# Spreading one row over 128 partitions: from a selector matmul to two DMAs by way of DRAM

## The chip, the cores and the metric

The kernel runs on one core of one Trainium2 chip. The metric is device time in microseconds (us) of one execution. The kernel before was timed three times: 608.44, 608.82 and 608.91 us, median 608.82. A separate profiled execution of the same kernel took 607.33 us.

The five engines of the core have the short names of the profile: PE (TensorE, with its weight loads as PEld), DVE (VectorE), ACT (ScalarE), POOL (GpSimd) and SP (SyncE, which here only issues stores). DMAs are issued by POOL, SP and ACT, each from its own queue.

## What is computed

```python
X = np.fft.fft(x, axis=1)          # x: 8 x 3008 x 256, float32
X = np.fft.fft(X, axis=2)
t = X.real.reshape(8 * 3008, 256)
h = np.maximum(t @ w_in, 0.0)      # w_in: 256 x 2048
return (h * h) @ w_out             # w_out: 2048 x 256
```

A real two-dimensional Fourier mixing, then a feed-forward layer with a squared ReLU.

## The kernel before

**Folding the transforms.** Both transforms are sums of cosines and sines of real data, so the kernel computes row k and row S-k of the output together: the cosine part is common, the sine part changes its sign. `zc` holds the cosine part of such a pair and `zs` the sine part, both 128 partitions (index d of the model dimension) by columns (the pairs k). The transform over d is multiplied into `w_in` once, which gives the weights `gh[:, 0]` (for `zc`), `gh[:, 1]` (for `zs`) and `gh[:, 2]` (minus two times `gh[:, 1]`). There are 129 cosine indices d and 128 partitions; the sine of d = 0 is zero, so partition 0 of `zs` carries the cosine row d = 128 instead. That row must not change its sign with the rest, and this is what the change is about.

**Windows and steps.** The 12,040 pair columns are cut into 25 windows, most of 512 columns. A window w is worked off in eight steps s = 0 to 7 (`NST`), each of which makes two of the sixteen 128-row chunks of h for both rows of every pair. In every step PE also runs 16 matmuls of line 687 (`ffn2_steps`), the second product of the window before; its results are copied by ACT (L702) and stored by SP (L667). Some jobs of the next windows are spread over the steps by hand: the matmuls of line 572 that make `zc` and `zs` of the next window (`z_steps`, run in steps `lo` to `hi - 1`), their evacuation by ACT (L577, L583) and DVE (L601), and the folds of x on DVE. The program is written out in the order in which each engine executes it; nothing reorders it.

**Two kinds of step.** In an ordinary step PE makes cosine plus sine part (L829, L830), ACT applies the ReLU (L861) for row k, PE adds `gh[:, 2]` times `zs` (L852), and ACT applies the ReLU for row S-k. In a step that is listed in `diff[w]` (steps 4 and 6 at first, then mostly 0, 2, 4, 6; the windows of the folds have fewer) the second row comes without the extra matmuls:

1. PE makes the cosine part alone (L838, `cosines`).
2. DVE computes t2 = n2 - 2 times the cosine part (L842, `twice`).
3. PE adds the sine part in place (L847, `sines`), which must wait for `twice`, as both use the same PSUM tile.
4. ACT takes the ReLU for row k (L861), and DVE adds t2 for row S-k (L859).

Here `n2` is the correction for d = 128: the row in partition 0 of `zs`, spread over all 128 partitions as tile `zn`, times one number per row of h (`g2n`). POOL makes it (L790, `nyq_rows`, two instructions for a step).

**The spread.** `spread_nyq(wt)` makes `zn` for window wt. It multiplies `zs` by the 128 x 128 matrix `sel`, which is 1 in row 0 and 0 elsewhere (L781, one matmul of up to 512 columns into a `ps_z` tile), and ACT copies the result to SBUF (L782). It is called 21 times, once for each of windows 4 to 24, from `nyq` (L892) near the end of the window before, at step `hi`; `hi` is 5 when window w+1 has 0 in its list, else 6. Window 4 makes its own in step 0. `nyq_rows` for the first listed step follows in the same step, those for the others in the steps after. The `n2` tiles share three buffers. POOL's queue also holds the write of the folded rows to DRAM (L456), their read-back (L464, L466) and the loads of x (L127, L132), in the program's order.

Of the kernel before, what the change touches and what calls it, by code (L numbers as in the profile page):

```python
# [9 lines left out]
F32 = mybir.dt.float32  # L10
F16 = mybir.dt.float16
I32 = mybir.dt.int32
AF = mybir.ActivationFunctionType
# [3 lines left out]
P = 128  # L17
# [12 lines left out]
def kernel(  # L30
# [14 lines left out]
    nc = tc.nc  # L45
    B, S, D = x.shape
# [9 lines left out]
    WN = 512  # L56
# [25 lines left out]
    def win_of(col):  # L82
        return max(w for w in range(NW) if wins[w][0] <= col) if col < TOT else NW
# [5 lines left out]
    col_of = {}  # L89
# [11 lines left out]
    const = ctx.enter_context(tc.tile_pool(name="const", bufs=1))  # L101
# [9 lines left out]
    drp = ctx.enter_context(tc.tile_pool(name="drp", bufs=2, space=bass.MemoryType.DRAM))  # L111
    ps_h = ctx.enter_context(tc.tile_pool(name="ps_h", bufs=2, space=bass.MemoryType.PSUM))
    ps_o = ctx.enter_context(tc.tile_pool(name="ps_o", bufs=2, space=bass.MemoryType.PSUM))
    ps_z = ctx.enter_context(tc.tile_pool(name="ps_z", bufs=2, space=bass.MemoryType.PSUM))
# [201 lines left out]
    for i in (1, 0):  # L316
        nc.gpsimd.tensor_scalar(out=perm[i], in0=prow_i, scalar1=float(P - 1 - i), scalar2=None, op0=ALU.is_equal)
    nc.gpsimd.dma_start(out=wout16, in_=moe_w_out.rearrange("(c p) o -> p c o", p=P))
    sel = const.tile([P, P], F16, name="sel")
    nc.gpsimd.memset(sel, 0.0)  # L320
    nc.gpsimd.memset(sel[0:1, :], 1.0)
    pick = const.tile([P, 1], F16, name="pick")
    nc.gpsimd.memset(pick, 0.0)
    nc.gpsimd.memset(pick[0:1, :], -2.0)
# [42 lines left out]
    def fold_steps(i):  # L367
# [130 lines left out]

        late = [lambda: fold8(0), lambda: fold8(1), lambda: fold16(0), lambda: fold16(1), nyq8]
        return {"u_odd": u_odd, "u_part": u_part, "v_even": v_even, "v_part": v_part, "d_even": d_even, "n_cos": n_cos, "odds": odds, "d_odd": d_odd, "load": load, "n_sin": n_sin, "nyq": nyq, "even": even, "away": away, "back": back, "late": late}  # L500

    gh = const.tile([P, 3, F], F16, name="gh")
# [35 lines left out]
    def zwin(w):  # L538
        if w not in zc:
            zc[w] = zp.tile([P, WN], F16, name="zc", tag="zc")  # L540
            zs[w] = zp.tile([P, WN], F16, name="zs", tag="zs")
        return zc[w], zs[w]
# [182 lines left out]
    NST = NFC // 2  # L725
    at_of = {w: [[] for _ in range(NST)] for w in range(NW)}
    post_of = {w: [[] for _ in range(NST)] for w in range(NW)}
    diff = {w: (0, 2, 4, 6) if w > 5 else (4, 6) for w in range(4, NW)}
# [35 lines left out]
    n2s = {}  # L764
# [12 lines left out]
    def spread_nyq(wt):  # L777
        wn1 = wins[wt][1]
        zn = zns[wt] = znp.tile([P, WN], F16, name="zn", tag="zn")
        pn = ps_z.tile([P, 512], F32, name="pn", tag="pz")  # L780
        nc.tensor.matmul(pn[:, 0:wn1], sel, zwin(wt)[1][:, 0:wn1], start=True, stop=True)  # L781
        nc.scalar.activation(zn[:, 0:wn1], pn[:, 0:wn1], AF.Copy, bias=0.0, scale=1.0)  # L782

    def nyq_rows(wt, steps):
        wn1 = wins[wt][1]
        for s in steps:
            n2 = n2s[wt, s] = wp.tile([P, 2, WN], F32, name="n2", tag="w16")
            for a in range(2):
                fc = 2 * s + a
                nc.gpsimd.tensor_scalar(out=n2[:, a, 0:wn1], in0=zns[wt][:, 0:wn1], scalar1=g2n[:, fc : fc + 1], scalar2=1.0, op0=ALU.mult, op1=ALU.mult)  # L790

    old = None
    for w in range(NW):
# [1 line left out]
        h2 = h2p.tile([P, NFC, 2 * WN], F16, name="h2", tag="h2")  # L795
        zcw, zsw = zwin(w)

        lo, hi = int(any(win_of(col_of[i, 1]) == w + 1 for i in range(2, B))), NST - 3 if 0 in diff.get(w + 1, ()) else NST - 2
        at, post = at_of[w], post_of[w]
        if w == 1:  # L800
            fj = fold_jobs(1)
# [6 lines left out]
        elif w == 3:  # L808
# [4 lines left out]
            lo, hi = 3, NST - 1  # L813
        elif w == win_of(col_of[1, 1]) - 1:
            for st in range(5):
                at[min(st, 3)] += folds[1]["late"][st : st + 1]
            lo, hi = 4, NST - 1
# [74 lines left out]
        def nyq(s):  # L892
            if w + 1 in diff and hi < NST - 1:
                if s == hi:
                    spread_nyq(w + 1)
                    nyq_rows(w + 1, diff[w + 1][0:1])
                elif s == hi + 1:
                    nyq_rows(w + 1, diff[w + 1][1 : 2 if s < NST - 1 else None])
                elif s == hi + 2:
                    nyq_rows(w + 1, diff[w + 1][2:])  # L900
            if s == 0 and w in diff and w not in zns:
                spread_nyq(w)
                nyq_rows(w, diff[w])

        def quad(p):
            ph = phs[p] = ps_h.tile([P, 2, 512], F32, name="ph", tag="psh")
            for c in range(4):
                f0 = (4 * p + c) * P
                o = ph[:, c // 2, (c % 2) * wn : (c % 2 + 1) * wn]
                nc.tensor.matmul(o, gh[:, 0, f0 : f0 + P], zcw[:, 0:wn], start=(c % 2 == 0), stop=False, skip_group_check=True)  # L910
                nc.tensor.matmul(o, gh[:, 1, f0 : f0 + P], zsw[:, 0:wn], start=False, stop=True, skip_group_check=True)
# [54 lines left out]
        for s in range(NST) if w > 1 else ():  # L966
            held["on"] = s + 1 in diff.get(w, ()) or (s + 1 == NST and 0 in diff.get(w + 1, ()))
            if s in diff.get(w, ()):
                cosines(s)
                twice(s)  # L970
                settle()
                others(s)
                sines(s)
                first(s)
                relu(s, 1)
                keep(s, 1, 2)
                plus.append(lambda s=s, p=power_act: p(s))
                nyq(s)
                continue
            pq(s)  # L980
            settle()
            first(s)
            if s == NST - 1:
                power(s, 0, 1)
            others(s)
            nyq(s)
            turn(s)
            relu(s, 1)
            keep(s, int(s == NST - 1), 2)
# [36 lines left out]
```

## Time and profile before

| | |
|---|---|
| timed, median of three | 608.82 us |
| profiled execution, its own time | 607.33 us |
| its span | 605.5 us |
| PE busy | 591.2 us, 98% of the span |
| DVE, ACT, POOL busy | 490.1, 462.8, 213.6 us |
| mean granted TensorE clock | 0.999 |
| spread matmuls (L781) | 21, median 379 ns each |
| their copies (L782, ACT) | 21, median 608 ns each |
| rows of n2 (L790, POOL) | 146, median 692 ns, longest 2444 ns |

The duration of a matmul in the profile is that of one instruction from its start to its modelled end. Matmuls are pipelined, so the rate is read from the distance between the starts of two that follow each other: 0.21 us for 512 columns.

### The profile page before, as it was taken

How to read it: one execution, taken by the hardware profiler on the slowest of the kernel's cores; microseconds unless marked ns; L12 is line 12 of the kernel's file. 1: busy time of each engine (PE TensorE's matmuls, PEld its weight loads, DVE VectorE, ACT ScalarE, POOL GpSimd, SP SyncE). 2: the span in 40 equal slices, each digit the busy share in tenths (PEclk: the TensorE clock that was granted, in tenths of full speed). 3: DMA queues.
4: the chain of work that ended last, by engine and by line, in shares of the span. 5: the costliest groups of instructions: out<-in, count | busy, mean ns of one | idle time of the engine just before them, and what ended most of it. 6: DMA issues, size and time to landing. Idle time of an engine off the chain costs nothing.

```text
span 605.5 us, 11294 instructions
## 1 busy us (share of the span) xinstructions
PE 591.2 (98%) x4449; PEld 427.9 (71%) x4449; DVE 490.1 (81%) x593; ACT 462.8 (76%) x634; POOL 213.6 (35%) x249
## 2 busy tenths in 40 slices
PE   7899999999999999999999999999999999999997
PEld 3457786776777777777777767777677777777786
DVE  8787656987998878979889799888988988777760
ACT  6697777968888787877787878787777787878762
POOL 8320223245504506365045451363431522513300
PEclk9999999999999999999999999999999999999999
DMA  8945321127111361271113711146112311111112
GB/s 150 155 90 136 115 71 34 39 94 150 52 49 40 114 140 52 77 166 48 52 37 109 146 53 36 40 125 134 44 30 86 88 35 39 51 46 38 54 57 69
DMA packets 36524, 47.52 MB, mean 78 GB/s; under 512 B 4215, under 2 KB 30327, under 8 KB 36471
## 3 DMA queue, kind: packets, MB, share of 16 engines
q0 software_dynamic: 9344, 22.14, 17.9%
q1 hardware_dynamic: 26899, 24.44, 13.5%
q8 instruction: 35, 0.57, 0.4%
q10 hardware_dynamic: 228, 0.21, 0.1%
q14 instruction: 18, 0.15, 0.1%
HBM read 33.63 MB, written 27.84 MB: 102 GB/s over the span
## 4 chain that ended last, share of the span: by engine, by line
PE 87%; DVE 9%; ACT 2%; issue 1%; POOL 0%; DVEq 0%; POOLq 0%; ACTq 0%
PE po L687 49%; PE ph L852 8%; PE ph L829 7%; PE ph L830 7%; PE ph L847 5%; PE ph L838 5%; PE pz L572 4%; DVE h L868 3%; DVE t L842 2%; DVE h L859 2%; DVE xy L491 1%; PE pn L781 1%; ACT h L923 1%; ACT h L861 0%; DVE m L243 0%
## 5 line engine op out<-in xcount | busy, mean ns | idle before, releaser
L687 PE MATMUL po<-wout,h 128*128 128x256 f16 (+1 forms) x3024 | 362.3, 273 | 0.0
L861 ACT ACTIVATE h<-ph 128x1024 f16<-128x1024 f32 (+3 forms) x311 | 295.5, 993 | 79.0 <-PE ph L847 59.1
L687 PEld LDWEIGHTS <-h 128*128 128x128 f16 (+1 forms) x3024 | 296.8, 98 | 72.0
L790 POOL TENSOR_SCALAR n<-zn,g2n 128x512 f32<-128x512 f16 (+2 forms) x146 | 144.2, 1002 | 256.3 <-ACT zn L782 248.4
L868 DVE TENSOR_TENSOR h<-h 128x1024 f16<-128x1024 f16 (+6 forms) x216 | 203.2, 951 | 30.0 <-ACT h L861 27.5
L859 DVE CUSTOM_DVE_ANT_0 h<-t,ph 128x1024 f16<-128x1024 f32 x67 | 81.7, 1220 | 31.6 <-ACT h L861 31.5
L842 DVE SCALAR_TENSOR_TENSOR t<-ph,n 128x1024 f32<-128x1024 f32 (+2 forms) x73 | 87.7, 1202 | 23.4 <-PE ph L838 22.1
L829 PE MATMUL ph<-zc,gh 128*128 128x512 f16 (+3 forms) x238 | 87.4, 368 | 0.4 <-ACT h L923 0.3
L830 PE MATMUL ph<-zs,gh 128*128 128x512 f16 (+3 forms) x238 | 87.4, 368 | 0.0
L872 ACT ACTIVATE h<-h 128x1024 f16<-128x1024 f16 (+2 forms) x73 | 76.5, 1048 | 0.0
L852 PE MATMUL ph<-zs,gh 128*128 128x512 f16 (+3 forms) x238 | 68.1, 368 | 0.2 <-ACT h L861 0.2
L702 ACT ACTIVATE osb<-po 128x512 f32<-128x512 f32 (+3 forms) x95 | 55.5, 589 | 10.6 <-PE po L687 9.7
L847 PE MATMUL ph<-zs,gh 128*128 128x512 f16 (+2 forms) x146 | 42.7, 374 | 1.4 <-DVE t L842 1.2
L838 PE MATMUL ph<-zc,gh 128*128 128x512 f16 (+2 forms) x146 | 42.8, 375 | 0.4 <-DVE h L859 0.4
L830 PEld LDWEIGHTS <-gh 128*128 128x128 f16 x238 | 23.2, 98 | 25.7 <-issue 0.9
L829 PEld LDWEIGHTS <-gh 128*128 128x128 f16 x238 | 23.2, 97 | 25.0
L577 ACT ACTIVATE es<-pz 128x376 f32<-128x376 f32 (+1 forms) x32 | 14.9, 486 | 16.4 <-PE pz L572 16.3
L852 PEld LDWEIGHTS <-gh 128*128 128x128 f16 x238 | 22.3, 98 | 6.2 <-issue 0.3
L838 PEld LDWEIGHTS <-gh 128*128 128x128 f16 x146 | 14.3, 98 | 17.2 <-issue 0.6
L456 POOL DMA_DIRECT2D scr<-ev x8 | 4.9, 616 | 58.3 <-DVE ev L452 52.5
L466 POOL DMA_INDIRECT rb<-scr,idx_r x16 | 18.2, 1140 | 4.9 <-issue 4.9
L132 POOL DMA_INDIRECT xo<-in_x_dram,idx_r x15 | 16.3, 1090 | 4.5 <-issue 4.3
(145 smaller groups left out, 368.5 us busy)
## 6 DMA issues: line engine op xcount, KB each, us to landing
out_dram<-osb SPq DMA_DIRECT2D x77, 128.0 KB
xo<-in_x_dram POOLq DMA_DIRECT2D x7, 768.0 KB
scr<-ev POOLq DMA_DIRECT2D x8, 390.0 KB, 2.9
rb<-scr POOLq DMA_DIRECT2D x16, 130.0 KB
out_dram<-osb SPq DMA_DIRECT2D x12, 94.0 KB
w<-in_moe_w_in_dram POOLq DMA_DIRECT2D x2, 512.0 KB
wout<-in_moe_w_out_dram POOLq DMA_DIRECT2D x1, 1024.0 KB, 11.9
out_dram<-osb SPq DMA_DIRECT2D x8, 75.0 KB
```

The source lines that it names most:

```text
L687: nc.tensor.matmul(po[0:m, j * D : (j + 1) * D], h2[:, fc, q : q + m], wout16[:, fc, :], start=(fc == 0), stop=(fc == NFC - 1))
L790: nc.gpsimd.tensor_scalar(out=n2[:, a, 0:wn1], in0=zns[wt][:, 0:wn1], scalar1=g2n[:, fc : fc + 1], scalar2=1.0, op0=ALU.mult, op1=ALU.mult)
L829: nc.tensor.matmul(ph[:, a, 0:wn], gh[:, 0, f0 : f0 + P], zcw[:, 0:wn], start=True, stop=False)
L830: nc.tensor.matmul(ph[:, a, 0:wn], gh[:, 1, f0 : f0 + P], zsw[:, 0:wn], start=False, stop=True)
L838: nc.tensor.matmul(ph[:, a, 0:wn], gh[:, 0, f0 : f0 + P], zcw[:, 0:wn], start=True, stop=True)
L842: nc.vector.scalar_tensor_tensor(out=t2[:, :, 0:wn], in0=phs[s][:, :, 0:wn], scalar=-2.0, in1=n2s[w, s][:, :, 0:wn], op0=ALU.mult, op1=ALU ...
L847: nc.tensor.matmul(phs[s][:, a, 0:wn], gh[:, 1, f0 : f0 + P], zsw[:, 0:wn], start=False, stop=True, skip_group_check=True)
L852: nc.tensor.matmul(phs[s][:, a, 0:wn], gh[:, 2, f0 : f0 + P], zsw[:, 0:wn], start=False, stop=True, skip_group_check=True)
L859: nc.vector._custom_dve(TENSOR_ADD_SAT, out=h, in0=t2s[s][:, :, 0:wn], in1=phs[s][:, :, 0:wn], s0=BIG, s1=0.0)
L861: nc.scalar.activation(h, phs[s][:, :, 0:wn], AF.Relu, bias=0.0, scale=-1.0)
L868: nc.vector.tensor_tensor(h, h, h, op=ALU.mult)
L872: nc.scalar.activation(h, h, AF.Square, bias=0.0, scale=1.0)
```

## The change

`sel` goes. `spread_nyq` writes the row (1 x 512 f16, 1 KB) from partition 0 of `zs` to a DRAM tile `rd` with a DMA on ACT's queue, and a DMA on POOL's queue reads that row back into all 128 partitions of `zn`, with a stride of 0 over the partitions. POOL's DMA waits for the landing of ACT's, and `nyq_rows` for the landing of POOL's.

The calls move as well. `hi` becomes one smaller wherever window w+1 has `diff` steps: 4 (0 in its list) or 5. The spread comes at step `hi`, the first `nyq_rows` at `hi + 1`, the second at `hi + 2`, the rest at `hi + 3`; what doesn't fit into the window is made in step 0 of the next. As `hi` also ends the stretch over which the matmuls of line 572 are spread, these are now done one step earlier, in four steps in place of five (three or four where `lo` is 1).

```diff
-    sel = const.tile([P, P], F16, name="sel")
-    nc.gpsimd.memset(sel, 0.0)
-    nc.gpsimd.memset(sel[0:1, :], 1.0)
...
     def spread_nyq(wt):
         wn1 = wins[wt][1]
         zn = zns[wt] = znp.tile([P, WN], F16, name="zn", tag="zn")
-        pn = ps_z.tile([P, 512], F32, name="pn", tag="pz")
-        nc.tensor.matmul(pn[:, 0:wn1], sel, zwin(wt)[1][:, 0:wn1], start=True, stop=True)
-        nc.scalar.activation(zn[:, 0:wn1], pn[:, 0:wn1], AF.Copy, bias=0.0, scale=1.0)
+        rd = drp.tile([1, WN], F16, name="rd", tag="rd")
+        nc.scalar.dma_start(out=rd[:, 0:wn1], in_=zwin(wt)[1][0:1, 0:wn1])
+        nc.gpsimd.dma_start(out=zn[:, 0:wn1], in_=bass.AP(tensor=rd.tensor, offset=rd.offset, ap=[[0, P], [1, wn1]]))
...
-        lo, hi = int(any(win_of(col_of[i, 1]) == w + 1 for i in range(2, B))), NST - 3 if 0 in diff.get(w + 1, ()) else NST - 2
+        lo, hi = int(any(win_of(col_of[i, 1]) == w + 1 for i in range(2, B))), NST - 4 if 0 in diff.get(w + 1, ()) else NST - 3 if w + 1 in diff else NST - 2
...
             if w + 1 in diff and hi < NST - 1:
                 if s == hi:
                     spread_nyq(w + 1)
+                elif s == hi + 1:
                     nyq_rows(w + 1, diff[w + 1][0:1])
-                elif s == hi + 1:
-                    nyq_rows(w + 1, diff[w + 1][1 : 2 if s < NST - 1 else None])
                 elif s == hi + 2:
+                    nyq_rows(w + 1, diff[w + 1][1:2])
+                elif s == hi + 3:
                     nyq_rows(w + 1, diff[w + 1][2:])
             if s == 0 and w in diff and w not in zns:
                 spread_nyq(w)
                 nyq_rows(w, diff[w])
+            elif s == 0 and w in diff:
+                nyq_rows(w, [q for q in diff[w] if (w, q) not in n2s])
```

## The prediction

> **What bounds the kernel now.** I read the page first: the busy times and the chain of work that ended last.
>
> ```profile
> PE 591.2 (98%) x4449; PEld 427.9 (71%) x4449; DVE 490.1 (81%) x593; ACT 462.8 (76%) x634; POOL 213.6 (35%) x249
> ...
> PE po L687 49%; PE ph L852 8%; PE ph L829 7%; PE ph L830 7%; PE ph L847 5%; PE ph L838 5%; PE pz L572 4%; DVE h L868 3%; DVE t L842 2%; DVE h L859 2%; DVE xy L491 1%; PE pn L781 1%; ACT h L923 1%; ACT h L861 0%; DVE m L243 0%
> ```
>
> PE carries the chain, and the selector matmul stands in it with 1%. A busy PE need not be at its rate, so next the sums of the stretch that holds every spread, 90 to 590 us, and then the order of time around one selector matmul.
>
> ```profile
> 90.00:590.00 500.00, 497.95 (x3759) 361.46 (x3758) 421.57 (x479) 392.28 (x528) 184.15 (x194) 1.00 0.27 71
> ```
>
> The second time is PE's: idle for 2.05 us of 500, at a granted clock of 1.00.
>
> ```profile
> 301.42 0.59 PE L847 MATMUL ph<-zs,gh 128*128 128x512 f16 x2
> 301.63 0.10 PEld L781 LDWEIGHTS <-sel 128*128 128x128 f16 x1
> 301.85 0.38 PE L781 MATMUL pn<-zs,sel 128*128 128x512 f16 x1
> ...
> 302.06 0.38 PE L829 MATMUL ph<-zc,gh 128*128 128x512 f16 x1
> ...
> 302.28 0.38 PE L830 MATMUL ph<-zs,gh 128*128 128x512 f16 x1
> ```
>
> Matmuls of 512 columns start 0.21 us apart, the selector's among them. So PE is at its rate, and what leaves its queue leaves the time, as long as nothing new makes it wait.
>
> The waits say what could. POOL waits long for `zn`, DVE nearly never for POOL.
>
> ```profile
> POOL n L790 <- ACT zn L782: 248.4, 21, 18.6
> ...
> DVE t L842 <- PE ph L838: 22.1, 39, 0.9
> ...
> POOL n L790 <- DVE t L842: 7.4, 8, 2.2
> ...
> PE ph L847 <- DVE t L842: 1.2, 2, 0.6
> ```
>
> **What the change removes.** Nineteen selector matmuls of 512 columns, one of 448, one of 360: 21 x 0.21 = 4.4 us off PE (the shorter two take 0.1 off that; the chain's 0.7%, unrounded, of 605.5 is 4.2). Their weight loads lie under other matmuls (71% busy). The 21 copies of 0.61 us, 12.7 us of ACT, free nothing: ACT idles over 100 us. `sel`'s two memsets lie at the start behind the load of `w_out`; no view shows anyone waiting for them.
>
> **What it adds on ACT and the DMA queues.** Twenty-one issues on ACT. The only row of ACT issuing a DMA is the tail's, 257 to 527 ns, so 21 x 0.33 = 6.9 us against the 12.7 saved. The issue follows the first ReLU (L861) of its step and is ahead of the next one: queued behind it are L872, L702 and the second ReLU, for which PE waits in the end. It waits for `zs`. In window 13 DVE's last write of `zs` (L601) ends at 321.34 and the ReLU at about 322.1, so it holds nothing up there. It also waits for the store eight DMAs earlier, as completion counters are taken in turn; stores were issued 7 to 26 us ahead of these points, and only one had not clearly landed. Bounds for this wait: 0 to 1.5 us in one window, inside ACT's idle gaps of 0.95 and 1.7 us below. I take 0. SP's stores also find the counters shifted by one; SP waits 410 us for ACT, so 0. The traffic is 21 x 129 KB, 2.7 MB beside 47.5.
>
> **What it adds on POOL: is `n2` still in time?** This is the open term. The tightest place is step 0 of a window that has 0 in its list, fourteen of the 21. Window 14:
>
> ```profile
> 321.05 1.98 ACT L861 ACTIVATE h<-ph 128x1024 f16<-128x1024 f32 x2
> 322.86 1.10 ACT L872 ACTIVATE h<-h 128x1024 f16<-128x1024 f16 x1
> 323.81 0.65 ACT L702 ACTIVATE osb<-po 128x512 f32<-128x512 f32 x1
> 324.28 0.66 ACT L782 ACTIVATE zn<-pn 128x512 f16<-128x512 f32 x1
> 324.76 1.10 ACT L861 ACTIVATE h<-ph 128x1024 f16<-128x1024 f32 x1
> 326.81 1.94 ACT L861 ACTIVATE h<-ph 128x1024 f16<-128x1024 f32 x2 [0.95 <-PE ph L847]
> ```
>
> ```profile
> 318.90 0.64 POOL L456 DMA_DIRECT2D scr<-ev  x1 [9.06 <-DVE ev L452]
> 325.12 1.36 POOL L790 TENSOR_SCALAR n<-zn,g2n 128x512 f32<-128x512 f16 x2 [5.58 <-ACT zn L782]
> 326.43 1.14 POOL L464 DMA_DIRECT2D rb<-scr  x2
> ```
>
> ```profile
> 330.35 1.23 DVE L842 SCALAR_TENSOR_TENSOR t<-ph,n 128x1024 f32<-128x1024 f32 x1
> ```
>
> Now POOL's two rows end at 326.5 and DVE uses them at 330.35: 3.9 us to spare. The new write is issued behind the first ReLU of step 4, at 322.1 at the latest, 2.2 us ahead of where ACT's copy started. For the write the nearest rows are the one-row loads of lines 157 and 155, whose completions in the trace's semaphore records come 1.9 and 3.5 us after the issue (`scr`, a write of 390 KB, 2.9). For the read it is L464, the same kind of DMA on the same queue with 130 KB: ten of sixteen had landed by 2.3 us after the issue, two by 3.0, four took 4.4 to 5.4. I take 1.9 and 2.2, the majority. 322.1 + 1.9 + 0.1 + 2.2 + 1.4 (two rows) = 327.7. DVE is ready at 330.35 - 0.21 = 330.1, as the selector is gone: 2.4 us to spare. In the fourteen windows the ReLU ends 8.1 to 9.4 us ahead of that use, so 2.3 to 3.5 are left. Cost 0. The upper end is 3.5 + 5.4: 332.5, 2.4 us late. Every late 0.1 us is 0.1 us of PE, since L847 follows L842 with only 0.25 us to spare. A gain from this path is excluded, nobody waits for `n2` now (0.5 us once).
>
> The other rows keep their places or have 4.6 us and more. POOL's queue behind the waiting DMA moves about 1.2 us back (327.7 against 326.5): the read-back L464/L466 and then the load of x, which DVE needs a window later. The load of x, landing some 11 us after its issue, would end just before the spread of windows 12, 15 and 18 starts, and is not in its way.
>
> [...]
>
> **What it moves on PE.** The matmuls of line 572 come one step earlier, so step 4 of the windows that make a new `zs` loses about 0.4 us of filler (2.4 matmuls of 0.157 us spacing) between L838 and L847. Steps without filler show 0.25 us between the end of `twice` and L847, steps with it 0.5 to 0.7, so the margin stays positive where DVE is not behind. Where it is behind with folds PE already stalls 0.24 to 0.75 us. Bounds: 0, and 14 x 0.38 = 5.3. Present stalls of this kind come to about 3.6 us by the starts of the matmuls, over 73 such steps: 0.05 each. 14 x 0.05 = 0.7, nearest to the lower end, as most margins are measured there. Four or five of L601's copies now come ahead of L859 in step 4; in window 13 L859 waits for ACT until 322.14 anyway.
>
> **Sum.** -4.4 + 0 + 0 + 0.7 = -3.7. The profiled execution, 607.33 (span 605.5 and 1.8 around it), would take 603.6. It lay 1.5 below the median of the timed runs, 608.82, and against that I forecast 605.1.
>
> **Rivals.**
>
> - *A, slower: the rows come too late in step 0.* One read in four was slow; with a slow write too, 3.5 of the fourteen windows are 2.4 us late: +8.4, 613.5. For it: both slow pairs of L464 fell behind a write of `scr` and amid stores, as these reads do. Against: 2.3 us and more to spare with the majority. It decides from 0.35 us late per window on average (4.9 of 14).
> - *B, slower: `z` in four steps crowds DVE and PE.* All of the filler lost: 605.1 - 0.7 + 5.3 = 609.7, more if DVE falls behind for a step. Against: the margins of 0.25 us that most steps without filler show.
> - *C, no change: the gain is given back.* Only the read is slow: 322.1 + 1.9 + 0.1 + 5.4 + 1.4 = 330.9, 0.8 late, 3.5 x 0.8 = 2.8: 607.9.
> - That PE keeps its time though the matmuls go (another engine being the bound) is part of C: DVE and ACT are idle 78 and 108 us of the 500, and PE 2.
>
> **How the numbers follow.** A run of this kernel can tell about 0.2% (1.2 us) from no change. Forecast 0.62, A 0.15, C 0.14, B 0.09 (B mostly slower by over 0.2% with what it brings for DVE, at times no change). The likeliest alone spans 603.6 (no new stall, and the lower edge of the timed runs) to 607.5. The range goes to 611, which takes in C, most of B and the milder half of A. Faster 0.62, same 0.15, slower 0.23.
>
> **What would show it.** In the changed kernel's profile: PE's busy time down by 4 us and the selector gone from the chain; the write landing about 2 us and the read 2.2 to 3 us after their issues; DVE's wait for POOL's `n` still under 1 us in all (over 4 us is A); the idle time of PE from 90 us to the end at 2 to 3 us (above 6 with `twice` as releaser is B). The prediction is wrong if one of the two transfers takes over 4.5 us in most windows, or if ACT is held at its issue for more than its next idle gap.

## The result, and the profile after

The changed kernel takes 614.95 us (median of six, 613.65 to 616.57) and the kernel before 608.58 us (median of six, 607.96 to 608.91): a ratio of 1.0106 [1.0087, 1.0124]. The forecast was 605.1. It is slower, by about what rival A gave (613.5). The profiled execution took 615.95 us, its span is 614.2. In the changed kernel most lines have a number smaller by three: `twice` is L839, `sines` L844, the rows of `n2` L787, the ReLU L858; the write of `rd` is L778 and the read of `zn` L779.

First the page of the changed kernel: the busy times and the chain of work that ended last.

```profile
PE 588.8 (96%) x4428; PEld 426.1 (69%) x4428; DVE 484.9 (79%) x593; ACT 453.0 (74%) x613; POOL 217.1 (35%) x268
...
PE 73%; DMA 13%; DVE 7%; ACT 2%; issue 2%; POOL 2%; POOLq 0%; DVEq 0%; ACTq 0%
PE po L684 42%; PE ph L826 6%; PE ph L849 6%; PE ph L827 6%; DMA zn<-rd 6%; DMA rd<-zs 5%; PE ph L844 5%; PE ph L835 4%; PE pz L569 3%; DVE t L839 2%; DMA out_dram<-osb 2%; POOL n L787 1%; DVE h L865 1%; DVE h L856 1%; ACT h L858 1%
```

The selector is gone from the chain, and PE's busy time is down by 2.4 us. But the two new transfers now stand in it with 6% and 5%: in some windows the end of the kernel hangs on them and not on PE. The sums of the stretch from 90 to 590 us (PE's busy time is the second number) say the same:

```profile
90.00:590.00 500.00, 487.27 (x3670) 352.90 (x3667) 411.18 (x473) 377.43 (x501) 187.59 (x215) 1.00 0.30 76
```

PE idles 12.73 us of the 500, at a granted clock of 1.00; before it was 2.05. Who makes it wait stands in the waits (total, times, longest):

```profile
POOL n L787 <- DMA zn<-rd: 78.7, 21, 5.2
...
DVE t L839 <- POOL n L787: 16.1, 12, 2.5
...
PE ph L844 <- DVE t L839: 10.5, 9, 2.1
...
ACT h L858 <- DMA out_dram<-osb: 2.0, 1, 2.0
```

DVE's wait for POOL's rows went from 0.5 us to 16.1, and PE's wait for `twice` from 1.2 to 10.5. Read from the starts of its matmuls, PE stalls 13.1 us more than before. Eight stalls lie between `twice` and `sines`, one each in windows 7, 11, 12, 14, 15, 17, 18 and 23 (2.30, 1.86, 1.14, 0.57, 0.83, 1.54, 1.59, 1.81: 11.6 us), one of 1.74 lies elsewhere and is told below, and the others are 0.3 less than before. With the 4.4 us of matmuls that are gone, 13.1 - 4.4 = 8.7 us: the spans differ by 614.2 - 605.5 = 8.7.

A late window in the order of time, window 23 (start, duration, then the instruction; in brackets the idle time ahead of it and who ended it):

```profile
546.33 1.02 ACT L858 ACTIVATE h<-ph 128x1024 f16<-128x1024 f32 x1 [1.00 <-PE ph L844]
546.75 0.22 ACTq L778 DMA_DIRECT2D rd<-zs  x1
547.25 1.02 ACT L858 ACTIVATE h<-ph 128x1024 f16<-128x1024 f32 x1
...
550.81 0.59 POOL L779 DMA_DIRECT2D zn<-rd  x1 [14.46 <-DMA rd<-zs]
556.14 3.80 POOL L787 TENSOR_SCALAR n<-zn,g2n 128x512 f32<-128x512 f16 x5 [4.74 <-DMA zn<-rd]
...
557.53 1.22 DVE L839 SCALAR_TENSOR_TENSOR t<-ph,n 128x1024 f32<-128x1024 f32 x1 [1.94 <-POOL n L787]
```

ACT issues the write at 546.75, POOL can issue the read only 4.06 us later, the rows start 5.33 us after that, and DVE is held for 1.94 us. In a window where the transfers are quick (window 21 of the same run) the two steps take 1.61 and 3.48 us and DVE doesn't wait.

Why is a write of 1 KB slow? The DMA view of that stretch (40 slices of 0.1 us: tenths of the 16 engines in use, then GB/s, and below the DMAs issued in it):

```profile
DMA  4432211000000000000000000000000000000000
GB/s 164 143 113 82 72 51 51 21 20 31 20 20 31 20 20 31 20 21 31 20 20 31 20 31 20 20 31 20 20 21 31 20 31 20 20 0 0 0 0 20
...
out_dram<-osb SPq DMA_DIRECT2D x1, 121.0 KB
out_dram<-osb SPq DMA_DIRECT2D x1, 41.0 KB
rd<-zs ACTq DMA_DIRECT2D x1, 1.0 KB
out_dram<-osb SPq DMA_DIRECT2D x1, 7.0 KB
```

From 547.2 to 549.9 the DMA side runs at a steady 20 to 31 GB/s with a tenth of its engines in use or less. That is one engine moving one output row of 1 KB after the other (a packet is 46 ns long and the next starts 42 ns after its start, which is 24 GB/s), while the others are done. The write waits in line with those rows. The three stores in this view are issued at 549.7 us and later, behind that tail; the rows of the tail are from the stores issued from 543.5 to 545 us:

```profile
out_dram<-osb SPq DMA_DIRECT2D x1, 121.0 KB
out_dram<-osb SPq DMA_DIRECT2D x1, 87.0 KB
out_dram<-osb SPq DMA_DIRECT2D x1, 41.0 KB
out_dram<-osb SPq DMA_DIRECT2D x1, 7.0 KB
```

The packet records show it directly; below is my reading of them, not a view of the profile. A packet counts as "directly ahead" when the next one starts within 5 ns of its end; the two are then taken to be on the same engine (the records name no engine):

```
window   write issued   its packet starts   packets directly ahead of it, back to back
 13         305.70            +0.71          none
 21         499.70            +0.70          none
 19         453.39            +3.22          71 rows of 1 KB
 23         546.75            +3.22          76 rows of 1 KB
 11         252.84            +3.62          23 rows of 1 KB, 6 pieces of 6 KB (the write of scr)
```

Over the 21 windows the packet starts 0.70 to 0.72 us after the issue in seven, 1.0 to 1.4 in three and 2.5 to 4.3 in eleven. Why rows pile up on one engine can be read from the completions of the stores. In this trace a store of 41 rows is reported by 1 completion, one of 87 rows by 3, of 7 rows by 7, of 121 rows by 11 and of 128 rows by 16 (where there are fewer than 16, one more comes early, mostly 0.4 to 0.6 us after the issue, and is not counted here). In 298 of the 314 stores their number is the largest divisor up to 16 of the count of rows; the other 16 stores show fewer. I take each completion for one engine with an even share of the rows, which is my reading, not a record. SP stored 41, 87, 7 and 121 rows just ahead of window 23's write. If one engine has a share of all four, it gets 41 + 29 + 1 + 11 = 82 rows, and the write, a single row with one completion, would wait behind them there. The trace agrees: counted back at 42 ns a row from the write's packet at 3.22 us, the 11, 1, 29 and 41 rows begin at 2.75, 2.70 and 1.47 us after the write's issue and 0.26 us before it, and at each of these borders the records show a small packet that reports a store as done. Of the 82 rows, 76 lie behind the issue.

The ninth stall is ACT's. In window 7 the issue of the write itself was held:

```profile
151.96 1.02 ACT L858 ACTIVATE h<-ph 128x1024 f16<-128x1024 f32 x1 [0.51 <-PE ph L844]
154.77 0.22 ACTq L778 DMA_DIRECT2D rd<-zs  x1
155.03 1.02 ACT L858 ACTIVATE h<-ph 128x1024 f16<-128x1024 f32 x1 [2.05 <-DMA out_dram<-osb]
```

ACT waits 2.05 us for the landing of a store, because the new DMA takes its completion counter over, and PE then waits 1.74 us for ACT's ReLU. In the trace the counter that both use is semaphore 117; the store has 53 rows, was issued at 144.92 and lands only at 154.75.

### The profile page after: what moved, and what is told of

Read it like the earlier page. It is cut to its first block, busy times and chain, and to the rows that moved or that the text cites. A ratio compares the mean times of both kernels' runs of the same rounds, so it can differ in the third digit from the quotient of the medians.

```text
span 614.2 us, 11257 instructions
## 1 busy us (share of the span) xinstructions
PE 588.8 (96%) x4428; PEld 426.1 (69%) x4428; DVE 484.9 (79%) x593; ACT 453.0 (74%) x613; POOL 217.1 (35%) x268
## 4 chain that ended last, share of the span: by engine, by line
PE 73%; DMA 13%; DVE 7%; ACT 2%; issue 2%; POOL 2%; POOLq 0%; DVEq 0%; ACTq 0%
PE po L684 42%; PE ph L826 6%; PE ph L849 6%; PE ph L827 6%; DMA zn<-rd 6%; DMA rd<-zs 5%; PE ph L844 5%; PE ph L835 4%; PE pz L569 3%; DVE t L839 2%; DMA out_dram<-osb 2%; POOL n L787 1%; DVE h L865 1%; DVE h L856 1%; ACT h L858 1%
## 5 line engine op out<-in xcount | busy, mean ns | idle before, releaser
L858 ACT ACTIVATE h<-ph 128x1024 f16<-128x1024 f32 (+3 forms) x311 | 294.9, 990 | 101.4 <-PE ph L844 79.2
L865 DVE TENSOR_TENSOR h<-h 128x1024 f16<-128x1024 f16 (+6 forms) x216 | 197.7, 926 | 29.6 <-ACT h L858 26.9
L787 POOL TENSOR_SCALAR n<-zn,g2n 128x512 f32<-128x512 f16 (+2 forms) x146 | 135.3, 940 | 79.8 <-DMA zn<-rd 78.7
L839 DVE SCALAR_TENSOR_TENSOR t<-ph,n 128x1024 f32<-128x1024 f32 (+2 forms) x73 | 87.7, 1202 | 37.7 <-PE ph L835 21.1
L779 POOL DMA_DIRECT2D zn<-rd x21 | 12.3, 584 | 198.3 <-DMA rd<-zs 198.3
L844 PE MATMUL ph<-zs,gh 128*128 128x512 f16 (+2 forms) x146 | 42.8, 374 | 10.8 <-DVE t L839 10.5
L827 PEld LDWEIGHTS <-gh 128*128 128x128 f16 x238 | 23.2, 98 | 25.7 <-issue 0.9
L826 PEld LDWEIGHTS <-gh 128*128 128x128 f16 x238 | 23.2, 97 | 25.0
L849 PEld LDWEIGHTS <-gh 128*128 128x128 f16 x238 | 22.3, 98 | 5.8 <-issue 2.1
L835 PEld LDWEIGHTS <-gh 128*128 128x128 f16 x146 | 14.3, 98 | 16.9 <-issue 0.3
L844 PEld LDWEIGHTS <-gh 128*128 128x128 f16 x146 | 13.7, 97 | 15.8 <-issue 13.2
```

Source lines behind the costliest of these rows:

```text
L826: nc.tensor.matmul(ph[:, a, 0:wn], gh[:, 0, f0 : f0 + P], zcw[:, 0:wn], start=True, stop=False)
L827: nc.tensor.matmul(ph[:, a, 0:wn], gh[:, 1, f0 : f0 + P], zsw[:, 0:wn], start=False, stop=True)
L835: nc.tensor.matmul(ph[:, a, 0:wn], gh[:, 0, f0 : f0 + P], zcw[:, 0:wn], start=True, stop=True)
L839: nc.vector.scalar_tensor_tensor(out=t2[:, :, 0:wn], in0=phs[s][:, :, 0:wn], scalar=-2.0, in1=n2s[w, s][:, :, 0:wn], op0=ALU.mult, op1=ALU ...
L844: nc.tensor.matmul(phs[s][:, a, 0:wn], gh[:, 1, f0 : f0 + P], zsw[:, 0:wn], start=False, stop=True, skip_group_check=True)
L849: nc.tensor.matmul(phs[s][:, a, 0:wn], gh[:, 2, f0 : f0 + P], zsw[:, 0:wn], start=False, stop=True, skip_group_check=True)
```

## The experiments

The theory from this profile (L): the rows are late because the two transfers take longer than they were given, and nothing else costs time. The rival (Z): moving line 572's matmuls and the spread a step earlier crowds PE and DVE.

**The changed kernel without the spread.**

```diff
-        zn = zns[wt] = znp.tile([P, WN], F16, name="zn", tag="zn")
...
+        zns[wt] = zn0          # a constant tile of zeros
```

> The changed kernel without the two DMAs of the spread: zn is one constant tile, set to zero at the start, so the correction for d = 128 is left out; all calls, steps and rows of n2 stay where the change put them. Theory L (the rows of n2 are late in step 0, because the two transfers take longer than the 2.4 us to spare, and PE waits for them): the waits go and the 4.4 us of the selector matmuls are gained, 608.6 - 4.4 = 604.2 us (603.6 to 605.0). Rival Z (doing the matmuls of line 572 in four steps in place of five crowds DVE and PE): the time stays at 611 us or above. Rival A (ACT is held at its DMA issue): also 604.2, so this run parts L and A from Z.

Measured: 603.44 us against 607.85, 0.9931 [0.9914, 0.9947]. All that is left is the new places without the matmuls, and the gain is 4.4 us, as expected: the price of the matmuls. Its sums from 90 to 590 us show PE as busy as it was before (497.95):

```profile
90.00:590.00 500.00, 498.20 (x3779) 363.58 (x3777) 412.21 (x482) 384.75 (x512) 196.12 (x188) 1.00 0.28 72
```

So the new places of line 572's matmuls cost nothing measurable, and all that the changed kernel loses against 603.4 comes with the two DMAs.

**Only the places, or only the DMAs.** First the selector matmul at the new places (the line of `hi` is shown against the kernel before; the calls of `nyq_rows` stand where the change put them, too):

```diff
-        lo, hi = ..., NST - 3 if 0 in diff.get(w + 1, ()) else NST - 2
+        lo, hi = ..., NST - 4 if 0 in diff.get(w + 1, ()) else NST - 3 if w + 1 in diff else NST - 2
```

> The selector matmul and ACT's copy put back, everything else as in the changed kernel: the calls one step earlier, line 572 in four steps. Theory L: the kernel before with other places, 608.6 us (607.8 to 609.4). Rival Z: what the places cost shows here, 612 us or above. Together with the run without a spread this gives the price of the 21 matmuls, by L 4.4 us.

Measured: 612.5 us, 1.008 [1.0063, 1.0097]: not L's number, and the one that Z gave, but not for Z's reason. The waits of this kernel:

```profile
PEld L781 <- PE ph L847: 6.0, 4, 1.5
...
PE pn L781 <- DVE zs L601: 5.0, 5, 1.0
```

At the new place DVE has not written the last columns of `zs` when PE reaches the selector, so PE itself stands still, 5.8 us in all, read from the starts of its matmuls. In the kernel without the spread these stalls don't exist at the same places, so this is no crowding by line 572: the selector can't go that early, whereas none of PE's waits in the changed kernel is for a DMA.

Then the two DMAs in the kernel before, at the old places:

```diff
-        nc.tensor.matmul(pn[:, 0:wn1], sel, zwin(wt)[1][:, 0:wn1], start=True, stop=True)
-        nc.scalar.activation(zn[:, 0:wn1], pn[:, 0:wn1], AF.Copy, bias=0.0, scale=1.0)
+        nc.scalar.dma_start(out=rd[:, 0:wn1], in_=zwin(wt)[1][0:1, 0:wn1])
+        nc.gpsimd.dma_start(out=zn[:, 0:wn1], in_=bass.AP(tensor=rd.tensor, offset=rd.offset, ap=[[0, P], [1, wn1]]))
```

> One part of the change alone: the two DMAs in place of the selector matmul, but the calls, hi and the rows of n2 where the kernel before has them. Theory L: the chain starts about 2.2 us later against the use of its rows than in the changed kernel, so nearly every one of the fourteen windows is late, by some 0.6 us where the write is fast (1.6 us) and 3 to 5 us where it is slow, about 32 us in all: 625 to 645 us. If lateness didn't pass on to PE one to one, below 620.

Measured (one run): 638.83 us, against a median of 608.73 for the kernel before. Nearly every window is late, by up to 4.2 us:

```profile
DVE t L842 <- POOL n L790: 32.5, 21, 4.2
...
PE ph L847 <- DVE t L842: 22.7, 16, 4.3
```

The 30 us are not all waits. This run's granted clock is 0.977, that of the kernel before 0.996 or 0.997 beside it. In the trace PE runs at half clock for 3.4 to 6.8 us at four places (from 167.9, 273.7, 423.9 and 454.6 us), each time from 2.5 to 3.3 us after the start of a stall of over 3 us. Read from the starts of the matmuls, this takes about 9.6 us, beside the 22.7 of waits for `twice`. One run doesn't show that the stall brings the slow clock; the order is the same all four times. So the DMAs need the earlier places, and in eight windows these are not early enough.

**The stores.** If the stores delay the transfers, other stores must cure it. First a kernel whose stores write contiguous rows, one DMA for each group (`cnt` is 128 in 180 of 194):

```diff
-        for b, k0, kstep, n, c0 in runs:
...
+        row = (S * B // 2 if minus else 0) + g0
+        cnt = min(m, (S * B if minus else S * B // 2) - row)
```

> The changed kernel with every store of a group as one DMA of whole contiguous rows (mostly 128) in place of two to five DMAs with row counts such as 71, 57, 37, 91: the rows of the output land in a wrong order and sixteen are left out, all the arithmetic stays. Theory L in its narrower form (the 1 KB write is one packet on one DMA engine, and waits there behind stores whose row counts put them on one or few engines): the write lands in about 1.6 us in nearly all windows, the read in under 3.5 us, and the time falls by 6 to 9 us, to 605 to 609. If the transfers are slow for another reason (the read of one row by 128 partitions, or HBM), the write still takes 3 to 5 us in half of the windows and the time stays within 2 us of 615.

> The kernel before with the same even stores, as the base of the run above (its output is in a wrong order too). Both theories: PE is the bound and nothing waits for stores, so 608.6 us (607.6 to 609.2). The changed kernel with even stores should be 3 to 4.4 us below this one by theory L.

Measured: 601.46 us, 0.9898 [0.9881, 0.9914], for the changed kernel with such stores, and 607.1, 0.9989 [0.9978, 1.0001], for the kernel before with them. Such stores are worth hardly anything to the kernel before (0.1%) and 2.1% to the changed one (1.0106 to 0.9898), 13 us. The last part of the read lands 3.2 to 3.65 us after its issue in all 21 windows, and DVE's wait for the rows is 0.6 us. The direction is theory L's, but the gain is larger than expected: 601.5 where 605 to 609 were named, and 5.6 us under the kernel before with the same stores in place of 3 to 4.4.

Next every row at its own place again, but each store cut at the last multiple of 16 rows.

```diff
-            eng.dma_start(out=... [[kstep * D, cnt], [1, D]] ..., in_=osb[lo : lo + cnt, :])
+            for r0, r1 in ((0, cnt // 16 * 16), (cnt // 16 * 16, cnt)):
+                if r0 < r1:
+                    eng.dma_start(out=... (row + kstep * r0) * D ... [[kstep * D, r1 - r0], [1, D]] ..., in_=osb[lo + r0 : lo + r1, :])
```

> The changed kernel with each store cut at a multiple of 16 rows (71 rows become 64 and 7), the output complete and in place. Theory L with its cause (stores of row counts such as 71 or 91 are carried by one or few DMA engines for microseconds, and whatever has a part on such an engine waits behind them): the rows are now shared by more engines, the write lands in 1.6 to 2.5 us and the read in under 4 us in nearly all windows, PE's waits for twice fall from 13.6 to under 4 us, and the time from 615 to 602 to 606 us, below the kernel before. If the stores hold the transfers by their number or bytes, not by where they run, there are more of them now and the time stays at 612 or above. More stores also use up the completion counters sooner: if ACT is held for that at its issue, PE waits for ACT and the time is 606 to 611.

> The kernel before, selector matmul and old places, with the stores cut at a multiple of 16 rows as in cut_stores. Theory L: nothing in the kernel before waits for a store's landing, so it stays at 608.6 us (607.6 to 609.2, or up to 0.9 us less, as the even stores gave), and the 7.2 us of cut_stores under the kernel before belong to the selector's matmuls and the places. If the cut itself is worth several us, 602 to 605.

Measured: **601.51 us, 0.9889 [0.9866, 0.9912]**, for the changed kernel with cut stores, and 607.47, 0.9982 [0.9969, 0.9996], for the kernel before with them. The first beats both kernels, though it issues 504 DMAs for its stores in place of 314; it lies 0.5 us below the range expected. Its page (the chain) and its sums from 90 to 590 us:

```profile
PE 90%; DVE 4%; ACT 3%; issue 1%; DMA 1%; SPq 0%; POOL 0%; ACTq 0%; POOLq 0%; DVEq 0%
```

```profile
90.00:590.00 500.00, 499.18 (x3784) 364.19 (x3782) 416.36 (x481) 384.39 (x512) 201.02 (x215) 1.00 0.31 78
```

No transfer of the spread is left in the chain, and PE idles 0.82 us of 500. Its waits show none of PE for `twice` and none of DVE for POOL's rows. Window 23 of this kernel, in the order of time:

```profile
534.74 0.20 ACTq L780 DMA_DIRECT2D rd<-zs  x1
...
536.38 0.58 POOL L781 DMA_DIRECT2D zn<-rd  x1 [13.40 <-DMA rd<-zs]
539.79 6.41 POOL L789 TENSOR_SCALAR n<-zn,g2n 128x512 f32<-128x512 f16 x7 [2.83 <-DMA zn<-rd]
...
543.84 1.21 DVE L841 SCALAR_TENSOR_TENSOR t<-ph,n 128x1024 f32<-128x1024 f32 x1
```

and its DMA side from 534.5 us on (again 0.1 us a slice; the write is issued in slice 3):

```profile
DMA  0010005899630000000000000000000450749233
GB/s 21 0 51 21 0 0 174 205 256 277 205 103 21 10 0 0 0 0 0 0 0 0 0 0 0 0 0 0 0 0 0 123 123 0 164 82 164 41 82 62
```

The stores issued ahead of the write are over in a short burst of 0.8 us on up to nine tenths of the engines, in place of a tail of nearly 3 us on one. The steps take 1.64 and 3.41 us against 4.06 and 5.33, and `twice` waits for nobody. In all 21 windows the write's packet starts 0.69 to 1.14 us after its issue. (Of the two row counts that the expectation names, 71 has one completion in the trace of the changed kernel, but 91 has thirteen.) The cause is therefore shown by an edit that touches neither the spread nor its places. Of the 7.2 us gained, 4.4 are the matmuls and 0.8 the cut stores' own; the remaining 2.0 I don't assign, they are about what the intervals leave open.

**Another way for the row.** Would one DMA straight from partition 0 of `zs` to `zn` be quicker than two by way of DRAM? Once on ACT's queue and once on POOL's:

```diff
-        rd = drp.tile([1, WN], F16, name="rd", tag="rd")
-        nc.scalar.dma_start(out=rd[:, 0:wn1], in_=zwin(wt)[1][0:1, 0:wn1])
-        nc.gpsimd.dma_start(out=zn[:, 0:wn1], in_=bass.AP(tensor=rd.tensor, offset=rd.offset, ap=[[0, P], [1, wn1]]))
+        zr = zwin(wt)[1][0:1, 0:wn1]
+        nc.scalar.dma_start(out=zn[:, 0:wn1], in_=bass.AP(tensor=zr.tensor, offset=zr.offset, ap=[list(zr.ap[0]), [0, P], [1, wn1]]))
```

> The changed kernel with one DMA in place of two, from partition 0 of zs straight into the 128 partitions of zn (source read with a stride of 0), on ACT's queue; all places as in the changed kernel. Theory L: only the sum of the two transfers was too long. One transfer spread over all DMA engines, 2.2 to 5 us after the issue by the rows of the read so far, leaves more than the 7.6 us needed in every window, so PE's waits for twice fall from 13.6 us to about 3, and the time is that without a spread, 603.4 us (602.9 to 605.0). If the stores hold even one transfer for more than 7 us now and then, up to 607. If ACT's issue itself cost PE, it would stay above 606.

> The same single DMA on POOL's queue. Theory L: 603.4 to 605.5 us, as above; POOL now waits for zs itself, and the rows of n2 that stand in front of it in its queue can delay the issue, so at most 1 us above the one on ACT's queue. A time above 608 would mean that what matters is POOL's place in line and not the transfer.

Measured: 612.5 us, 1.0065 [1.0039, 1.0091], on ACT's queue and 606.78, 0.997 [0.9956, 0.9984], on POOL's. Both are above what was expected. The main reason is the same: a direct DMA is one hop, but a slow one. Its row in the page of DMA issues of the kernel on POOL's queue (count, size, median us to landing):

```profile
zn<-zs POOLq DMA_DIRECT2D x19, 128.0 KB, 6.9
```

Its last part lands 5.2 to 8.4 us after its issue, 6.4 to 6.7 in most quiet windows, and 9.4 to 11.3 in windows 11 and 17, while the write and the read by way of DRAM need about 1.6 + 3.3 in quiet windows. POOL's version is better for more than one reason. In windows 11 and 17, the latest of both kernels, POOL issues 1.3 us sooner ahead of the use than ACT does. In window 7 ACT's issue is held, as in the changed kernel:

```profile
ACT h L857 <- DMA out_dram<-osb: 3.2, 1, 3.2
```

This costs PE 2.86 us. And the granted clock of ACT's version is 0.989 to 0.994, of POOL's 0.995 or more. What each is worth of the 5.7 us between the two was not separated.

Does it matter which queue carries the 1 KB write?

```diff
-        nc.scalar.dma_start(out=rd[:, 0:wn1], in_=zwin(wt)[1][0:1, 0:wn1])
+        nc.gpsimd.dma_start(out=rd[:, 0:wn1], in_=zwin(wt)[1][0:1, 0:wn1])
```

> Both DMAs of the changed kernel stay, by way of DRAM, but the 1 KB write is issued by POOL and not by ACT, so that it doesn't share a queue kind with SP's stores. Theory L in its narrower form: the write no longer stands behind the stores of odd row counts on the same DMA engine, lands in 1.6 to 2.2 us in nearly all windows, the read stays at 3.2 to 5.5, and most of the 9 us of new PE waits go: 604.5 to 608 us. If the slow write is a matter of HBM or of any small write, it stays at 3 to 5 us in half of the windows and the time at 613 or above.

Measured: 614.46 us, 1.0106 [1.0076, 1.0136]: no better than the change, and my expectation missed. The waits are nearly those of the changed kernel:

```profile
DVE t L839 <- POOL n L787: 16.6, 12, 3.2
...
PE ph L844 <- DVE t L839: 10.6, 7, 2.7
```

On POOL's queue the write has sixteen completions where ACT's has one, and it is landed only with the last of them: 1.6 to 1.8 us after its issue in quiet windows, 2.3 to 7.0 in busy ones. In the packet records it is sixteen pieces of 64 bytes. In window 23 fifteen of them start 1.1 to 1.3 us after the issue and the last at 2.77, so the one late piece holds the whole.

**More time instead of quicker transfers.** The same transfers one step earlier, the rows left where they were:

```diff
-        lo, hi = ..., NST - 4 if 0 in diff.get(w + 1, ()) else NST - 3 if w + 1 in diff else NST - 2
+        lo, hi = ..., NST - 5 if 0 in diff.get(w + 1, ()) else NST - 4 if w + 1 in diff else NST - 2
```

> The changed kernel with hi one smaller again (3 or 4) and the rows of n2 at their present steps: the two transfers get one step more, about 2.9 us, and line 572 one step less. Theory L: the rows were 0.3 to 2.4 us late, so nearly all PE waits for twice go: 603.4 to 606 us. Rival Z: three steps for line 572 crowd DVE and PE further, 612 us or above.

> The cut stores together with the spread one step earlier. By theory L either alone already takes away nearly all of the waits, so both together give what one gives, about 603 to 604.5 us; well below 603 would mean that the stores cost something else too.

Measured: 604.27 us, 0.9935 [0.9915, 0.9954], and with the cut stores as well 604.81, 0.994 [0.9924, 0.9957]. With a whole step more the slow transfers are in time, as theory L has it; the waits of the first of the two have only

```profile
PE ph L844 <- DVE t L839: 1.6, 7, 0.4
```

But with line 572's matmuls in three steps PE idles 2.54 and 2.78 us of the 500, and cutting the stores gains nothing more: this looks like rival Z, about 2 us against the 0.82 of the kernel with cut stores alone. It was not shown to be line 572, as no kernel has these places without the spread. Here the better cure is the quicker transfer, not the earlier one.

## Why the prediction was wrong, by its own steps

- **PE is the bound, and each matmul taken off its queue is time: right.** 4.4 us was forecast, and 607.85 - 603.44 = 4.4 was measured without the spread.
- **ACT's issue costs nothing: right but once.** It takes 0.22 us (the first 0.48), not 0.33, and goes out beside a ReLU (in window 23 in the middle of it). The wait for a completion counter was bounded at 1.5 us in one window and put at 0 as lying in idle gaps; it came in one window, lasted 2.05 us and cost 1.74.
- **`n2` is in time: this is the step that failed.** Its terms were "I take 1.9 and 2.2, the majority", which left 2.4 us to spare. The term that was mis-sized is the two transfers in the company of stores. Up to the read's issue it took 1.4 to 1.6 us in quiet windows but 3.3 to 5.5 in eleven of 21, and from the read's issue to its last part 3.2 at best and up to 5.7. The read's bound, 5.4, nearly held. The write's, 3.5, did not: it landed up to 4.95 us after its issue. That the most which the bounds gave, 2.4 us late, is so near DVE's longest wait of 2.5 is luck, as the stretch to fill was longer than assumed (next point). What was wrong was to count slow cases as one in four of the reads and as independent of the place: eight windows are late, those in which such stores go out just ahead of the spread, and window 7, where ACT's hold adds to it. In windows 19, 20 and 22 the write is slow too, but the rows come in time.
- **In quiet windows the slack came out nearly right, 1.86 us for 2.4, by errors that cancel.** Window 17 of the kernel with cut stores has 1.86 us to spare. From the issue to `twice` 9.3 us are available (8.0 was assumed: the issue goes at the start of the ReLU, not behind it). Of these the write and POOL's start take 1.83 (2.0 assumed), the read 3.34 to the rows' start (2.2), the two rows 2.30 (1.4). The read's row, L464, was read too low: none of its sixteen DMAs shows all sixteen completions in the trace (two to eleven), so their last one may be missing; the new reads show all sixteen. The other read of the same tile in the kernel before, L466, gives 3.1 to 5.2 us to landing.
- **The two rows** take 1.36 us in the five late windows where DVE stands still. With DVE at work they take anything from 1.35 to 3.8; in window 17 of the kernel with cut stores it is 2.30, where they start 0.15 us into a multiplication of DVE (L867, 1.22 us). What stretches them was not shown. The issues of the reads show no hold beside such multiplications: 538 to 625 ns in all 21.
- **Line 572 in four steps: 0.7 us was forecast, no cost was found.** Without the spread PE idles 1.8 us of the 500, against 2.05 before.
- **The rivals.** A's mechanism was named, with its turning point at 4.9 us of lateness in all; it came to 11.6, in eight windows of 1.5 us on average where A had 3.5 windows of 2.4. Its evidence was quoted in the prediction ("both slow pairs of L464 fell behind a write of `scr` and amid stores, as these reads do") and then not priced: the number of rows of each store around each spread stands in the trace of before and was not used. B was not seen at these places, C neither. The sign given for A, DVE's wait for `n` over 4 us, came (16.1). The sign for the step itself, a transfer of over 4.5 us in most windows, did not come (the read takes that long in eight of 21), so it was set too far out; ACT's hold beyond its next idle gap came once.

## What to carry to other kernels

A transfer that something waits for must be priced by what stands ahead of it on its DMA engines, in every window, and not by the majority of quiet cases: look at the sizes of the stores issued just before it. Here stores of 41, 87, 7 and 121 rows left a tail of nearly 3 us on one engine (window 23). Such stores cost next to nothing (0.2% in the kernel before) until a short DMA with a deadline came behind them; cutting them at a multiple of 16 rows turned this change from 1.1% slower into 1.1% faster. A job that is moved from a bound engine to slower transfers needs either that, or a place with a whole step to spare; here the second gave 604.3 us against 601.5.

## What was not expected of the hardware

- The single packet of a 1 KB write, 46 ns long when nothing disturbs it, can start up to 4.3 us after the issue in place of 0.7, behind as many as 76 rows of 1 KB, while at least nine tenths of the DMA engines' time is idle.
- Spreading one row from a single partition to 128 (128 KB) takes 6.4 to 6.7 us straight from SBUF to SBUF in most quiet windows, and 3.2 to 3.5 when it is read from DRAM. Why was not tried.
- Packets of 6 KB of POOL's write of `scr`, 0.24 us each by the median of 512, took 0.6 to 1.2 us just where stores trail beside them (windows 11, 14 and 17, one right ahead of window 17's write); with the cut stores the longest is 0.60. What holds such a packet stays open.
- In the run of the DMAs at the old places PE fell to half clock for 3.4 to 6.8 us, each time soon after a stall of over 3 us (four of four). The stalls of the changed kernel, 2.3 us at most, were followed by none, and of three of 2.8 to 2.9 us in the kernels with other ways for the row one was.
